# Reordering the opening of a fused clustered-attention and two-layer feed-forward kernel: squares, one-hot copies and a table load

## The chip, the cores and the metric

The kernel runs on one core of a Trainium2 chip. The metric is the device time of one execution in microseconds (us), smaller is better; the time given for a kernel is the median of several executions.

## The reference, cut to what matters

Clustered attention over 2 x 8 heads of 768 rows and 64 columns, then two feed-forward layers over the 1536 rows of 512 columns that the heads make up. Only the opening of the attention part is touched by the change.

```
q_n = q / (norm(q) + 1e-06);  k_n = k / (norm(k) + 1e-06);  c_n = centroids / (norm(centroids) + 1e-06)
q_assign = argmax(q_n @ c_n.T);  k_assign = argmax(k_n @ c_n.T)        # 16 centroids a head
mask = q_assign[:, None] == k_assign[None, :]
scores = where(mask, scale * q @ k.T, -1e9)
attn = exp(scores - max(scores));  attn = attn / (sum(attn) + 1e-09)
x = attn @ v                                                           # heads side by side: 1536 x 512
x = prelu(x @ w_in, alpha) @ w_out                                     # layer 1, d_ff 2048
x = rms_norm(x) * rms_g;  out = (silu(x @ w_gate) * (x @ w_val)) @ w_out2   # layer 2, d_ff 1536
```

## The kernel before

Heads are handled in eight pairs; q and k of a pair lie transposed in `raw[pr]` (128 partitions: two heads of 64 columns; index 0 is q, 1 is k; 768 rows each). Products that need full precision are made from a rounded part (`hi`) and its remainder (`lo`), which lie in `stages`. For each head two operand tiles are gathered by DMA: `op1` (partitions 0 to 63: `hi`; 64 to 79: a one-hot code of the row's cluster; 80 to 127: a part of `hi` of q and `lo` of k) and `op2`. A score tile on TensorE needs both; the one-hot rows make the mask, scaled by -2^60 on the q side.

Each engine works its instructions in the order in which the program writes them: an instruction that waits holds up all that stands behind it on its engine, and the DMAs issued by SyncE (SP) stand in one such order too. PSUM tiles named `ps_st` rotate through three buffers and `ps_pr` has one; a tile that gets a buffer again waits until the last reader of the tile before it is done. `ps_pv` and `ps_mx` have one buffer each, of two banks.

`setup` (L279 to L386) is the opening. It loads pairs 0 and 1 and does, for pair 0, everything up to the one-hot codes:

- roots of the centroids' sums of squares (`root`, tag `c`), transposed centroids (`spread`, L325, L328);
- squares of q and k (`prep_sq`, L469, ScalarE), `hi` and `lo` (`prep_hi` L608, `prep_lo` L614, VectorE);
- `warm` (L393): products of zeros, which only keep TensorE busy;
- `sims_mm` (L516): products of raw q and k with the centroids; `sims_copy` (L521) takes them out of PSUM, `sims_turn` (L527) transposes them back;
- `ss_rows` (L494): sums of squares by a product with ones, copied out (L496) and transposed (`ss_turn`, L503); `root` makes reciprocal norms of them: square root and an offset on ScalarE (L399, L400, and with `keep` a copy, L403), reciprocals on VectorE (L406 to L409);
- `prep_scale` and `prep_arg` (L543 to L565, VectorE): the argmax and the one-hot codes `oh`;
- the same products, sums and roots for pair 1, of which the VectorE part is left for later;
- a load of ScalarE's table set with the exponential (L376) and one small exponential (L378);
- `oht_direct(h)` (L577) for both heads of pair 0: 12 small products turn the codes into rows (L589; head 0 into `ps_pv` for k and `ps_mx` for q, head 1 into `ps_pr` and three `ps_st`), and ScalarE copies them into `op1` (k side L598, q side L600).

After that `plan` sets out slots from -12 on, each a list of steps sorted by a hand-written order. Slots -12 to -7 hold `max_tile` of phase 0: score products (L662) into `ps_pv` and `ps_mx` in turn, each followed by a maximum on VectorE (L666), with `max_split` (L671, L672) and `max_rows` (L690) behind; the first score tiles (`st_tile`, L712, L713, exponential L714) come in slots -7 and -5. In slot -12 SP also issues the second part of the operand gathers (`prep_dma_b(h, 2)`, L626, L630) and the loads of pair 2 (L454, L456).

Of the kernel before, what the change touches and what calls it, by code (L numbers as in the profile page):

```python
# [12 lines left out]
AF = mybir.ActivationFunctionType  # L13
ALU = mybir.AluOpType
# [4 lines left out]
BIG = float(2.0 ** 60)  # L19
# [170 lines left out]
def f(ap):  # L190
    return ap.bitcast(F32)
# [34 lines left out]
class Attention:  # L226
# [52 lines left out]
    def setup(self):  # L279

        nc, C, H, D = self.nc, self.C, self.H, self.D
        v, act, g = nc.vector, nc.scalar, nc.gpsimd
        n, rows = H * C, 2 * C
        cn = self.pre([n, 2, D], "cn")
        css = self.pre([n, 1], "css")
        self.sq0 = self.pre([128, D], "sq0")
        src = self.centroids.rearrange("h c d -> (h c) d")
        nc.sync.dma_start(out=cn, in_=src.unsqueeze(1).to_broadcast([n, 2, D]))
        for pr in range(2):
            for i in range(2, 4):  # L290
                self.load(pr, i)
        self.eps = self.pre([128, 2], "eps")
        self.hs = self.pre([128, 32], "hs")
        spare = self.pre([128, 1], "spare")
        for c, x in enumerate((1e-30, 1e-6)):
            g.memset(self.eps[:, c:c + 1], x)
        act.activation(out=spare, in_=self.eps[:, 0:1], func=AF.Sqrt)
        g.memset(self.cb0, 0.0)
        g.memset(self.hs, 0.0)
        for e in range(2):  # L300
            g.memset(self.hs[64 * e:64 * e + 64, e:e + 1], 1.0)
        g.memset(self.cb, 0.0)
        for t in self.mh:
            g.memset(f(t), 0.0)
        for c in range(C):
            g.memset(self.code[:, c:c + 1], float(C - c))
        pat = self.pre([128, 2 * C, 2, 2], "pat")
        g.memset(pat[:, :, 0], -BIG)
        g.memset(pat[:, :, 1], 1.0)
        for o2 in self.op2:  # L310
            g.memset(f(o2[64:66, 1, :]), 1.0)
        g.memset(self.ones, 1.0)
        g.memset(self.tiny, 1e-9)
        g.memset(self.low, 1.0)
        for i in range(4):
            g.memset(self.low[32 * i:32 * i + 1], 0.0)
        i = self.idf.rearrange("p (e g r) -> p g e r", e=2, r=32)
        hi, lo = (i[..., r:r + 1].to_broadcast([128, 2, 2, 64]) for r in range(2))
        g.tensor_tensor(out=self.sel, in0=hi, in1=lo, op=ALU.add)
        pat = pat.rearrange("p a i g -> p (a i g)")  # L320

        def spread(cb, w, copy):

            ps = self.bk.pr()
            nc.tensor.transpose(ps[:, :w], cn[:w].rearrange("p a d -> p (a d)"), self.idf[:w, :w])  # L325
            src = ps[:, :w].rearrange("p (j e c) -> p j e c", e=2, c=C)
            for e in range(2):
                copy(out=cb[64 * e:64 * e + 64, :, C * e:C * e + C], in_=src[64 * e:64 * e + 64, :, e, :])  # L328

        x = cn[:, 0, :]  # L330
        v.tensor_tensor_reduce(out=self.sq0[:n], in0=x, in1=x, scale=1.0, scalar=0.0, op0=ALU.mult, op1=ALU.add,
                               accum_out=css)
        steps, r = self.root(css, [n, 1], "c")
        self.warm(3, self.bk.pv)
        spread(self.cb0.unsqueeze(1), rows, v.tensor_copy)
        for step in steps:
            step()
        for i in range(2):
            self.prep_sq(0, i)
        self.prep_hi(0, 0)  # L340
        self.prep_lo(0, 0)
        for i in range(2):
            v.tensor_scalar(out=cn[:, i, :], in0=cn[:, i, :], scalar1=r, scalar2=None, op0=ALU.mult)
        self.prep_hi(0, 1)
        self.warm(6, self.bk.pv)
        rc = self.bk.st()
        for i in range(0, 128, rows):
            nc.tensor.matmul(rc[i:i + rows, 0:1], lhsT=self.idf[:rows, :rows], rhs=r[:rows], start=True, stop=True)
        act.copy(out=self.rc0, in_=rc[:, 0:1])
        ps = self.bk.pr()  # L350
        self.sims_mm(0, ps)
        self.prep_sq(1, 0)
        simc = self.sims_copy(0, ps, self.rc0)
        ssc = self.ss_rows(0, v.tensor_copy)
        for h in range(2):
            self.prep_dma_a(h)
        for h in range(2):
            self.prep_dma_b(h, 1)
        self.load_v(0)
        steps, rn = self.root(self.ss_turn(ssc), [128, self.T // 2, 4, 2], "n0")  # L360
        self.sims_turn(0, self.bk.st(), simc)
        spread(self.cb, n, act.copy)
        self.prep_sq(1, 1)
        for step in steps:
            step()
        self.norm[0] = None, rn
        self.prep_scale(0)
        for i in range(5):
            self.prep_arg(0, i)
        self.warm(3, self.bk.pv)  # L370
        ps = self.bk.st()
        self.sims_mm(1, ps)
        ssc = self.ss_rows(1, act.copy)
        self.simc[1] = self.sims_copy(1, ps, 1.0)
        self.norm[1] = self.root(self.ss_turn(ssc), [128, self.T // 2, 4, 2], "n1", True)
        act.add_instruction(mybir.InstLoadActFuncSet(name=nc.get_next_instruction_name(), act_func_set_id=EXP_AND_LN,  # L376
                                                     ins=[], outs=[]))
        act.activation(out=spare, in_=self.eps[:, 0:1], func=AF.Exp)  # L378
        self.warm(4, self.bk.pv)
        self.prep_lo(0, 1)  # L380
        for h in range(2):
            self.oht_direct(h)
        for i in range(2):
            self.prep_hi(1, i)
        v.tensor_tensor_reduce(out=pat, in0=pat, in1=self.idf, scale=1.0, scalar=0.0, op0=ALU.mult, op1=ALU.add,
                               accum_out=self.ohs)  # L386
# [190 lines left out]
    def oht_direct(self, h):  # L577

        nc, X = self.nc, self.T // 2
        if h:  # L580
            hi = [self.bk.pr(), self.bk.st()]
            ps = [[self.bk.st(), self.bk.st()], hi]
        else:
            ps = [b().rearrange("p a b -> p (a b)") for b in (self.bk.mx, self.bk.pv)]
            ps = [[b, b[:, self.HS:]] for b in ps]
        for i in (1, 0):
            for g in range(2):
                for x in range(X):
                    nc.tensor.matmul(ps[i][g][0:16, x * 128:(x + 1) * 128], lhsT=self.oh[0][:, x, h, :, i, g],  # L589
                                     rhs=self.idr, start=True, stop=True)  # L590
        o1 = self.op1[h][64:80]
        for i in (1, 0):
            cuts = ((0, 128), (128, self.S)) if not i else ((0, self.S),)
            parts = [(ps[i][g][:16, :self.HS], o1[:, i, sl]) for g, sl in self.halves()] if h else \
                [(ps[i][0][:16, a:b], o1[:, i, a:b]) for a, b in cuts]
            for src, dst in parts:
                if i:
                    nc.scalar.copy(out=dst, in_=src)  # L598
                else:
                    nc.scalar.activation(out=dst, in_=src, func=AF.Identity, scale=-BIG)  # L600

# [198 lines left out]
    def plan(self):  # L800
# [3 lines left out]
        def at(s, o, fn, *a):  # L804
            ev.setdefault(s, []).append((o, len(ev.get(s, [])), fn, a))
# [4 lines left out]
        for pr in range(self.NP):  # L810
# [8 lines left out]
                        at(b + to[0], to[1], fn, pr, n)  # L819
            h = 2 * pr  # L820
            if pr == 0:
                at(-12, -1, self.prep_dma_b, 0, 2)
                at(-12, 1, self.prep_dma_b, 1, 2)
            elif pr == 1:
                at(-5, 12, self.prep_dma_a, h)
                at(-4, 12, self.prep_dma_a, h + 1)
                at(5, 2.8, self.prep_dma_oh, h)
                at(5, 2.8, self.prep_dma_oh, h + 1)
                at(6, 2.8, self.prep_dma_b, h)
                at(6, 2.8, self.prep_dma_b, h + 1)  # L830
            else:
                for e in range(2):
                    at(b - 12, 2.5, self.prep_dma_a, h + e)
                    at(b - 12, 2.5, self.prep_dma_oh, h + e)
                    at(b - 11 + e, 2.5, self.prep_dma_b, h + e)
# [539 lines left out]
```

## Time and profile before

| | |
|---|---|
| time, median of 3 runs (lowest, highest) | 819.69 us (819.63, 819.71) |
| the profiled execution's own time | 819.63 us |
| its span in the profile | 817.9 us |
| instructions | 11705 |
| TensorE matmul busy | 809.6 us (99%) |
| VectorE busy | 623.7 us (76%) |
| ScalarE busy | 335.6 us (41%) |
| GpSimd busy | 362.1 us (44%) |

The span is the time between the first and the last recorded instruction; 1.7 us of the execution lie outside of it. A busy TensorE is one whose modelled matmul times leave no gap, and not one at its peak. Times of single rows are from the start of the span.

### The profile page before, as it was taken

The page shows a single profiled execution, that of the slowest core. Times are in us where ns is not written, and L with a number is a line of the kernel's source. Part 1 is how long each engine was busy: PE and PEld are TensorE (multiplying, and loading weights), DVE is VectorE, ACT ScalarE, POOL GpSimd, SP SyncE. Part 2 cuts the span into 40 slices and gives each one's busy share as a digit, 9 for nine tenths or more (in the row PEclk, how much of TensorE's full clock was granted, in tenths as well). Part 3 has the DMA queues.
Part 4 walks back from the last instruction along what each step waited for, and adds up shares of the span by engine and source line. Part 5 has one row for each costly group of instructions (what it writes and reads, how often), then busy time and mean ns, then how long its engine had stood idle before and what let it go on. Part 6 is the DMA issues. An engine that isn't in the chain of part 4 may idle for free.

```text
span 817.9 us, 11705 instructions
## 1 busy us (share of the span) xinstructions
PE 809.6 (99%) x4350; PEld 625.0 (76%) x4350; DVE 623.7 (76%) x1036; ACT 335.6 (41%) x652; POOL 362.1 (44%) x335
## 2 busy tenths in 40 slices
PE   8999999999999999999999999999999999999998
PEld 5565666666666888888888888888888888888887
DVE  6989999999998489999999977877555555555523
ACT  7655776666564333433434444432212221222110
POOL 3421221221213267786766772416465546554511
PEclk9999999999999999999999999999999999999999
DMA  8786655754532022232212220102121212121012
GB/s 206 201 229 181 132 154 161 171 111 115 133 114 79 1 77 78 78 103 65 88 59 75 77 78 1 51 1 78 52 77 54 76 52 77 57 73 51 1 52 103
DMA packets 23624, 74.03 MB, mean 91 GB/s; under 512 B 3600, under 2 KB 4752, under 8 KB 23568
## 3 DMA queue, kind: packets, MB, share of 16 engines
q1 hardware_dynamic: 23568, 73.29, 31.3%
q8 instruction: 34, 0.56, 0.3%
q14 instruction: 22, 0.18, 0.1%
HBM read 49.88 MB, written 3.15 MB: 65 GB/s over the span
## 4 chain that ended last, share of the span: by engine, by line
PE 96%; DVE 2%; DMA 1%; ACT 1%; issue 0%; SPq 0%; DVEq 0%; ACTq 0%
PE ps_st L1010 35%; PE ps_mx L1010 14%; PE ps_pv L1010 14%; PE ps_pv L728 8%; PE ps_pr L1010 5%; PE ps_st L712 4%; PE ps_st L713 4%; PE ps_sm L739 3%; PE ps_ma L662 3%; PE ps_mb L662 2%; DMA nat<-in_kn_dram 1%; DVE mx L666 1%; PE ps_pv L393 1%; PE ps_pr L516 1%; PE ps_pr L690 0%; PE ps_pr L782 0%
## 5 line engine op out<-in xcount | busy, mean ns | idle before, releaser
L1077 POOL TENSOR_TENSOR gl<-v,gh 128x512 fp32r<-128x512 f32 x68 | 96.0, 1412 | 143.8 <-ACT gh L1076 142.4
L1076 ACT CAST gh<-v 128x512 fp32r<-128x512 f32 x68 | 42.3, 622 | 151.9 <-DVE v L1073 83.3
L1073 DVE TENSOR_TENSOR v<-ps_st,t 128x512 f32<-128x512 f32 x36 | 24.9, 691 | 100.3 <-PE ps_st L1010 100.2
L714 ACT ACTIVATE p<-ps_st 128x384 f32<-128x384 f32 x192 | 85.3, 491 | 28.1 <-PE ps_st L713 26.6
L992 DVE SCALAR_TENSOR_TENSOR dec_a<-raw,dec_a 128x512 uint32<-128x512 uint32 x66 | 81.6, 1236 | 2.2
L728 PE MATMUL ps_pv<-p,vnat 128*64 128x384 f32 x384 | 72.6, 499 | 0.0
L1069 DVE SCALAR_TENSOR_TENSOR v<-v,alpha,t 128x512 f32<-128x512 f32 x45 | 53.0, 1177 | 21.9 <-ACT v L1068 21.8
L712 PE MATMUL ps_st<-op 128*128 128x384 f32 x192 | 67.8, 353 | 0.3 <-ACT oht L575 0.3
L1010 PE MATMUL ps_st<-x1h,stage 128*128 128x512 f32 x272 | 67.2, 389 | 0.0
L713 PE MATMUL ps_st<-op 82*128 82x384 f32 x192 | 65.0, 339 | 0.0
L1010 PEld LDWEIGHTS ps_st<-x1h,stage 128*128 128x128 f32 x272 | 51.1, 188 | 10.6
L1123 DVE TENSOR_TENSOR x<-ps_mx,x 128x1024 f32<-128x1024 f32 x36 | 43.9, 1220 | 18.7 <-PE ps_mx L1010 18.7
L664 DVE TENSOR_REDUCE mx<-ps_ma 128x1 f32<-128x384 f32 x90 | 49.7, 552 | 10.1 <-PE ps_ma L662 9.2
L798 POOL TENSOR_TENSOR x1l<-X,x1h 128x384 fp32r<-128x384 f32 x15 | 15.9, 1062 | 91.7 <-ACT x1h L795 91.7
L1010 PE MATMUL ps_st<-x1h,wvh 128*128 128x512 f32 x144 | 56.2, 390 | 0.0
L1010 PE MATMUL ps_st<-x1h,wvl 128*128 128x512 f32 x144 | 56.0, 389 | 0.0
L1010 PE MATMUL ps_st<-x1h,wih 128*128 128x512 f32 x132 | 51.6, 391 | 0.0
L1010 PE MATMUL ps_st<-x1h,wil 128*128 128x512 f32 x132 | 51.4, 389 | 0.0
L664 DVE TENSOR_REDUCE mx<-ps_mb 128x1 f32<-128x384 f32 x90 | 49.4, 549 | 0.1
L1123 DVE TENSOR_TENSOR x<-ps_pv,x 128x1024 f32<-128x1024 f32 x35 | 42.5, 1214 | 6.8 <-PE ps_pv L1010 6.8
L990 DVE TENSOR_SCALAR dec_a<-raw 128x512 uint32<-128x512 uint32 x66 | 47.6, 722 | 0.0
L995 DVE SCALAR_TENSOR_TENSOR dec_e<-raw,dec_e 128x512 f32<-128x512 uint32 x66 | 45.7, 692 | 2.3
(304 smaller groups left out, 1998.3 us busy)
## 6 DMA issues: line engine op xcount, KB each, us to landing
raw<-in_moe_w_out_dram SPq DMA_DIRECT2D x28, 512.0 KB, 3.5
op<-stage SPq DMA_DIRECT2D x32, 384.0 KB, 5.9
raw<-in_moe_w_in_dram SPq DMA_DIRECT2D x15, 512.0 KB, 3.6
raw<-in_moe_w_val_dram SPq DMA_DIRECT2D x12, 512.0 KB, 3.4
raw<-in_moe_w_gate_dram SPq DMA_DIRECT2D x12, 512.0 KB, 3.4
op<-stage SPq DMA_DIRECT2D x16, 288.0 KB, 5.9
raw<-in_qt_dram SPq DMA_DIRECT2D x8, 384.0 KB, 4.8
raw<-in_kt_dram SPq DMA_DIRECT2D x8, 384.0 KB, 5.1
```

Source lines behind the costliest of these rows:

```text
L664: nc.vector.tensor_reduce(out=mx[:, g, k:k + 1], in_=to, op=ALU.max, axis=AX.X)
L712: nc.tensor.matmul(ps, lhsT=o1[:, 1, ks], rhs=o1[:, 0, qs], start=True, stop=False)
L713: nc.tensor.matmul(ps, lhsT=o2[:, 1, ks], rhs=o2[:, 0, qs], start=False, stop=True)
L714: nc.scalar.activation(out=self.P[s][:, e], in_=ps, func=AF.Exp, scale=self.scale)
L728: nc.tensor.matmul(ps[64 * e:64 * e + 64], lhsT=self.vnat[ph // 2][:, e, t0 + y], rhs=P[y][:, e], start=t0 + y == 0, stop=t0 + y == T - 1)
L990: lambda: v.tensor_scalar(out=a, in0=top, scalar1=3, scalar2=0x3FFFFFFF, op0=ALU.logical_shift_left, op1=ALU.bitwise_and),
L992: lambda: v.scalar_tensor_tensor(out=a, in0=top, scalar=0xC0000000, in1=a, op0=ALU.bitwise_and, op1=ALU.bitwise_or),
L995: lambda: v.scalar_tensor_tensor(out=ef, in0=bot, scalar=2.0 ** -52, in1=ef, op0=ALU.mult, op1=ALU.mult),
L1010: self.nc.tensor.matmul(ps, lhsT=a, rhs=b, start=first and i == 0, stop=last and i == len(terms) - 1)
L1069: nc.vector.scalar_tensor_tensor(out=v, in0=v, scalar=self.nalpha[:, a], in1=t, op0=ALU.mult, op1=ALU.add)
L1077: nc.gpsimd.tensor_tensor(out=lo, in0=v, in1=f(hi), op=ALU.subtract)
L1123: nc.vector.tensor_tensor(out=dst, in0=ps, in1=dst, op=ALU.add)
```

## The change

For pair 0, the square of k is split: ScalarE squares the first 384 columns, VectorE the other 384. The sums of squares (`ss_rows(0)`) go to TensorE ahead of the products that spread the roots (L348) and of the centroids' products (`sims_mm(0)`), and ScalarE instead of VectorE copies them out. The scaling of the centroids moves from VectorE to ScalarE, `lo` of k from behind the one-hot codes to the first stretch of VectorE, the copy of the centroids' products (`sims_copy`) behind the roots' two ScalarE steps, and both squares of pair 1 behind the spread centroids. The second part of head 0's operand gather is issued ahead of the load of v. For the codes' rows: head 0's copies are split between ScalarE and VectorE and stand ahead of pair 1's roots, head 1's stand behind these roots (the second half of its k side on VectorE), and the table load comes after both.

```
--- before.py
+++ after.py
@@ setup
-        for i in range(2):
-            self.prep_sq(0, i)
-        self.prep_hi(0, 0)
-        self.prep_lo(0, 0)
-        for i in range(2):
-            v.tensor_scalar(out=cn[:, i, :], in0=cn[:, i, :], scalar1=r, scalar2=None, op0=ALU.mult)
-        self.prep_hi(0, 1)
+        self.prep_sq(0, 0)
+        self.prep_hi(0, 0)
+        sq, raw = self.nat[0][:, 1].rearrange("p t h d -> p (t h d)"), self.raw[0][:, 1]
+        (_, s0), (_, s1) = self.halves()
+        act.activation(out=sq[:, s0], in_=raw[:, s0], func=AF.Square)
+        v.tensor_tensor(out=sq[:, s1], in0=raw[:, s1], in1=raw[:, s1], op=ALU.mult)
+        self.prep_hi(0, 1)
+        for i in range(2):
+            act.activation(out=cn[:, i, :], in_=cn[:, i, :], func=AF.Identity, scale=r)
+        for i in range(2):
+            self.prep_lo(0, i)
         self.warm(6, self.bk.pv)
+        ssc = self.ss_rows(0, act.copy)
         rc = self.bk.st()
...
         self.sims_mm(0, ps)
-        self.prep_sq(1, 0)
-        simc = self.sims_copy(0, ps, self.rc0)
-        ssc = self.ss_rows(0, v.tensor_copy)
...
+        self.prep_dma_b(0, 2)
         self.load_v(0)
         steps, rn = self.root(self.ss_turn(ssc), [128, self.T // 2, 4, 2], "n0")
-        self.sims_turn(0, self.bk.st(), simc)
+        self.sims_turn(0, self.bk.st(), self.sims_copy(0, ps, self.rc0))
         spread(self.cb, n, act.copy)
-        self.prep_sq(1, 1)
+        for i in range(2):
+            self.prep_sq(1, i)
...
-        self.norm[1] = self.root(self.ss_turn(ssc), [128, self.T // 2, 4, 2], "n1", True)
+        ss = self.ss_turn(ssc)
+        self.warm(4, self.bk.pv)
+        self.oht_direct(0)
+        self.norm[1] = self.root(ss, [128, self.T // 2, 4, 2], "n1", True)
+        self.oht_direct(1)
         act.add_instruction(mybir.InstLoadActFuncSet(...))
         act.activation(out=spare, in_=self.eps[:, 0:1], func=AF.Exp)
-        self.warm(4, self.bk.pv)
-        self.prep_lo(0, 1)
-        for h in range(2):
-            self.oht_direct(h)
@@ oht_direct
+        cuts = (0, 128), (128, self.S)
         for i in (1, 0):
-            cuts = ((0, 128), (128, self.S)) if not i else ((0, self.S),)
-            parts = [(ps[i][g][:16, :self.HS], o1[:, i, sl]) for g, sl in self.halves()] if h else \
+            parts = [(ps[i][g][:16, :self.HS], o1[:, i, sl]) for g, sl in self.halves()] if h or i else \
                 [(ps[i][0][:16, a:b], o1[:, i, a:b]) for a, b in cuts]
-            for src, dst in parts:
+            for n, (src, dst) in enumerate(parts):
+                aside = n == (1 if i else 0) and (i or not h)
                 if i:
-                    nc.scalar.copy(out=dst, in_=src)
+                    (nc.vector.tensor_copy if aside else nc.scalar.copy)(out=dst, in_=src)
+                elif aside:
+                    nc.vector.tensor_scalar(out=dst, in0=src, scalar1=-BIG, scalar2=None, op0=ALU.mult)
                 else:
                     nc.scalar.activation(out=dst, in_=src, func=AF.Identity, scale=-BIG)
@@ plan
             if pr == 0:
-                at(-12, -1, self.prep_dma_b, 0, 2)
                 at(-12, 1, self.prep_dma_b, 1, 2)
```

## Rows read from the trace of the kernel before

**Rows 1.** The page, part 4: the chain that ended last, by engine.

```profile
PE 96%; DVE 2%; DMA 1%; ACT 1%; issue 0%; SPq 0%; DVEq 0%; ACTq 0%
```

**Rows 2.** The chain of waits, 0 to 60 us: start us, us, what.

```profile
3.33 2.86 PE ps_pv L393 x6
...
6.41 0.82 PE ps_pr L516 x8
7.22 0.70 PE ps_st L494 x8
...
8.56 0.55 PE ps_st L503 x3
...
13.71 1.28 ACT L376
...
15.24 0.79 ACT op L598
...
16.24 0.64 PE ps_pv L662 x2
...
16.90 2.70 DVE mx L666 x3
...
23.64 12.12 DMA nat<-in_kn_dram
...
36.65 0.47 ACT op L699
```

**Rows 3.** The timeline of ScalarE, 4 to 40 us: start, duration, instruction.

```profile
4.80 1.81 ACT L469 ACTIVATE nat<-raw 128x768 f32<-128x768 f32 x2 [1.12 <-DMA raw<-in_qt_dram]
...
7.72 0.56 ACT L521 ACTIVATE simc<-ps_pr,rc 128x384 f32<-128x384 f32 x1
...
9.46 0.32 ACT L400 ACTIVATE n_e<-n_y,eps 128x24 f32<-128x24 f32 x1
9.68 0.41 ACT L328 COPY cb<-ps_pr 64x64 f32<-64x64 f32 x2
10.11 0.84 ACT L469 ACTIVATE nat<-raw 128x768 f32<-128x768 f32 x1
11.89 0.48 ACT L496 COPY ssc<-ps_st 128x384 f32<-128x384 f32 x1 [0.94 <-PE ps_st L494]
...
13.54 0.16 ACT L403 COPY n_s<-ps_st 128x24 f32<-128x24 f32 x1
...
18.27 1.57 ACT L606 CAST stage<-raw 128x768 fp32r<-128x768 f32 x2
```

**Rows 4.** The timeline of VectorE, 4 to 30 us; in brackets the idle time before and its end.

```profile
7.95 0.56 DVE L496 COPY ssc<-ps_st 128x384 f32<-128x384 f32 x1 [0.47 <-PE ps_st L494]
9.46 0.30 DVE L406 RECIPROCAL n_a<-n_y 128x24 f32<-128x24 f32 x1 [0.95 <-ACT n_y L399]
```

**Rows 5.** The timeline of TensorE, 4 to 40 us: start, duration, instruction.

```profile
8.94 0.49 PE L527 MATMUL ps_st<-idf,simc 128*128 128x128 f32 x3
9.27 0.27 PE L325 MATMUL ps_pr<-idf,cn 128*128 128x128 f32 x1
...
12.72 1.17 PE L393 MATMUL ps_pv<-zero 128*128 128x512 f32 x4
14.21 0.52 PE L589 MATMUL ps_pv<-idr,oh 128*16 128x128 f32 x6 [0.31 <-DVE oh L565]
...
21.37 0.34 PE L712 MATMUL ps_st<-op 128*128 128x384 f32 x1
...
36.04 0.39 PE L690 MATMUL ps_pr<-idr,mh 128*64 128x128 f32 x3
```

**Rows 6.** Groups of instructions by line and shape, 4 to 24 us: ScalarE's L600.

```profile
L600 ACT ACTIVATE op<-ps_mx 16x640 fp32r<-16x640 f32 x1 | 0.7, 677 | 0.0
```

**Rows 7.** The timeline of SP's queue, 4 to 40 us.

```profile
15.47 0.56 SPq L626 DMA_DIRECT2D op<-stage  x1
```

**Rows 8.** Busy time by stretch, with granted clock, DMA share, GB/s at the end.

```profile
10.00:32.00 22.00, 19.69 (x132) 12.55 (x131) 19.53 (x45) 15.44 (x32) 5.50 (x11) 1.00 1.02 248
```

## Prediction

> **What bounds the kernel now.** I read the page's chain first, then the chain of waits over the first 60 us, then the timelines of the engines in the opening.
>
> The page puts 96% of the chain that ended last on TensorE [rows 1]. From about 39 us on its products follow each other to the end, and all engines work in written order. So what the opening gains or loses comes out at the end, less what later waits swallow. The reader should look at two things: when the first score product (L662) runs, and what swallows a shift behind it.
>
> The chain of the opening [rows 2]: zeros on TensorE from 3.33 to 6.19, centroids' products from 6.41, sums of squares from 7.22 to 7.92, a copy on VectorE at 7.95 [rows 4], transposes at 8.56. At the far end ScalarE loads the exponential's table at 13.71 for 1.28 us, copies head 0's code rows from 15.24, and the first score product starts at 16.24. The codes themselves were ready for TensorE at 14.21 [rows 5], so the copies began about 0.5 us after the first six products' end (14.73): that is what the load cost before. From 16.90 VectorE's maxima follow back to back, 0.9 us each. Then the chain shows a transfer from 23.64 to 35.76, the square that waited for it, and a row copy at 36.65.
>
> **The change, part by part.** All times are of the profiled execution (819.63 us, span 817.9); the median is 819.69, so its sums carry over as they are. What a measurement can tell from no change is about 0.2%, 1.64 us.
>
> *Pair 0's sums.* The two squares of 0.85 us ended at 6.61, so q is there at 4.80 and k at 5.76 [rows 3]. Half a square costs at most 0.48 on ScalarE (its copy of 384 columns [rows 3]) and 0.56 on VectorE [rows 4]: both halves are done by 6.33, when TensorE has just left the zeros (6.19). The sums take 0.70 plus at most 0.15 of waiting, to 7.0; ScalarE's copy ends at 7.5 instead of VectorE's at 8.52. But the products for the roots (0.22, from 6.19 to 6.41) and for the centroids (0.82) now stand between the sums and their transposes on TensorE: 7.0 + 1.04 = 8.0. The transposes start 0.55 earlier, not 1.0, and the root's second step (n_e) goes from 9.46 to 8.9.
>
> *VectorE's extra work.* It gets the half square (0.56) and `lo` of k (0.9 by the maxima of as many columns), 1.46 in all. It loses the copy (0.56) and the waits around it, 0.47 and 0.95 [rows 4], of which 1.43 are left when the reciprocal comes 0.55 earlier. The centroids' scaling leaves it too. So `lo` is hidden behind the wait for the square root; without that cover it would cost 0.9. I take 0; at worst 0.1.
>
> *The centroids' products.* Their copy now follows n_e, 0.22 after its start as L328 did before: 9.13, for 0.56 [rows 3], to 9.69 instead of 8.28. The transposes (0.49) end at 10.2, just when the roots are done, so VectorE's codes come 0.5 earlier: TensorE could have them at 13.7.
>
> *Pair 1.* Here the change pays. The transposes of the centroids end 0.6 after the start of the ones before [rows 5]: 10.3. Their two copies take 0.41, to 10.75 (before they began at 9.68). Both squares of pair 1 follow, 0.84 each with little overlap: 12.4, where before the second ended at 10.95 and the first lay in an earlier gap. The second half of pair 1's sums needs 0.35 to 0.5 more: 12.9, against 11.87. The copy and the transposes follow as before, 1.0 later, and the four products of zeros, which ended at 13.89, end at 14.9 [rows 5]. Only then come the code products: 14.9 instead of 14.21, although the codes are ready at 13.7.
>
> *Head 0's rows.* The six products for k end at 15.4 (0.52), the copies of both halves at 15.95 (0.56 the longer), the 128 columns of q on VectorE by 16.2, ScalarE's 640 (0.68 [rows 6]) at 16.5. The rows for the first score product are there at 16.2, as before. ScalarE is idle from about 13.8 to 15.4 now: the load and the small exponential (1.5) would have fitted in front of the copies. Moving them is worth nothing here.
>
> *Head 1's products.* They stand on TensorE ahead of the first score product, and the last three write the `ps_st` buffer that held pair 1's transposed sums. Its last reader is the copy L403, which now stands behind head 0's copies on ScalarE: 16.5, then 0.35 to n_e, 0.22 to L403, 0.16 [rows 2, 3], less 0.1 of overlap, is 17.1. The three products and the score product behind them follow: 17.3 instead of 16.24, 1.05 later. If that wait did not bind, TensorE would end the 24 products of 14.9 at 16.3 to 17.0 (each six between 0.35, an estimate from 0.52 less one product's run, and 0.52), so the shift lies between 0.1 and 1.05. I take the wait, since the order of the buffers and of ScalarE's steps is fixed by the text.
>
> *What lies behind.* The load is now between head 1's copies and the two casts of pair 1 (1.57 [rows 3]): about 18.3 to 19.8, casts to 21.4. The first score tile, 21.37 before, comes at about 22.4 and its exponential after it: hidden. The trace has the load at 1.28 us with the next instruction at its heels [rows 2]. The Trainium skill (ScalarE: Activation LUTs, What ACT_TABLE_LOAD costs) gives about 2.66 us for each switch, with a drain behind the load. By the page the casts would end near 22.8 and push the first rows' copy and exponential by about 1 us, to some 821.5; by the trace, which the sum follows, nothing.
>
> *Transfers.* Head 0's second gather goes from 15.47 [rows 7] to about 11, ahead of v. Its readers start at 21.37 before and 22.4 now; v is read later still. Nothing waits for either. All of SP's issues up to the casts of pair 1 come sooner, but the 16 DMA engines are at a share of 1.02 from 10 to 32 us [rows 8]: the end of this backlog moves only with its start, 0.3 to 0.7 earlier (`hi` of k comes that much sooner).
>
> *What swallows the shift.* The stretch from 16.9 to 36 is in order, so 1.05 arrives at 36: L690 ended at 36.43 [rows 5] and the row copy behind it waited for the late square until 36.65, which now is 0.2 of slack. 1.05 - 0.2 = 0.85 at the end: 819.69 + 0.85 = 820.5, span 818.7.
>
> **Rivals.**
> - *The buffer does not bind* or TensorE comes through pair 1 a little faster: a shift of 0.1 to 0.6 at the first score product, less 0.2: 819.6 to 820.1. For it: the trace of before shows no product that waits for L403, which ended at 13.70 there, before TensorE asked. Against it: the written order.
> - *The transfers set the stretch, on the other side.* The chain itself shows a transfer for 12.12 us up to 35.76. If the products have over 1 us of room in front of that square, the end follows the DMA backlog, 0.3 to 0.7 earlier: 819.0 to 819.4. It decides once products reach L690 no later than the square ends. Against it: L690 ended only 0.2 ahead of the row copy. The change would then do what its order suggests, at a size near the limit of measurement.
> - *TensorE's clock falls.* Its granted clock was 1.00 from 10 to 32 us [rows 8]; before 6.19 products of 512 columns took 0.48 each, later 0.29 or less [rows 2, 5]. TensorE now idles about 1.1 us (8.6 to 9.7) and 0.8 us (16.3 to 17.1), where the opening's chain had idled 0.64 at most between 6.19 and 9.1. If the clock fell, the some 5 us of products between 9.7 and 17.3 could take up to twice as long: 822 to 825. The Trainium skill (TensorE: Matmul & The Clock Gate, What's actually happening) says that the low level is the default and activity lifts it; no row before shows a fall.
> - *The load's place was the bound and pair 1 overlaps better than I sum*: first score product up to 0.9 earlier, 818.8 to 819.0, and not under 818 by any row.
>
> **How the numbers follow.** Forecast (0.5 to 1.1 later) 0.62; buffer not binding 0.15; transfers 0.12; clock or another wait 0.07; earlier first product 0.04. The likeliest gives 820.5. The range 819.2 to 821.2 leaves out the clock, the earlier product and half of the transfers' case, 0.17. Over 0.2% either way (under 818.05, over 821.33): faster 0.03; slower 0.09, from the clock and the forecast's tail; the rest, 0.88, within.
>
> **What would show it.** Right: transposes of pair 0's sums near 8.0; pair 1's second square ending near 12.4; ScalarE idle ahead of head 0's copies; TensorE waiting for ScalarE ahead of the last three code products; L662 near 17.3; the first table-bound exponential not waiting for the load; L699 near 37.5. Wrong: L662 before 16.2, or a slower TensorE product anywhere after 6.2 us, or a transfer that is waited for at 36 us with products idle.

## The result and the profile after

The changed kernel takes 825.01 us (median of 5, 824.60 to 825.15), the kernel before 819.71 us in the same job (819.63 to 821.00): 5.3 us more, a ratio of 1.006 with a 95% interval of 1.0047 to 1.0074. The span of the profiled execution went from 817.9 to 823.2 us. Lines have moved: the first score product L662 is L669 now, the row copy L699 is L706, the code copies L598 and L600 are L603, L605 and L607, the code products L589 are L593, sums of squares L494 are L498, the root's copy L403 is L407.

The page of the changed kernel, part 2: the span in 40 slices of 20.6 us, with the granted clock of TensorE in tenths.

```profile
PEclk9899999999999999999999999999999999999999
```

One slice is not at full clock: the second, from 20.6 us on. The stretches around it, from the same trace (granted clock is the third number from the end, DMA share the second):

```profile
17.30:19.20 1.90, 0.04 (x1) 0.04 (x2) 1.14 (x5) 1.42 (x5) 0.00 (x0) 1.00 0.95 246
19.20:20.60 1.40, 1.32 (x8) 0.93 (x8) 0.63 (x1) 1.40 (x4) 0.00 (x0) 1.00 1.12 206
20.60:27.50 6.90, 6.52 (x20) 5.86 (x21) 4.96 (x8) 3.17 (x5) 0.00 (x0) 0.51 1.02 305
```

TensorE was busy for 0.04 of 1.90 us ahead of 19.2; from 20.6 to 27.5 its granted clock was at the lower of its two levels (0.5, 1.2 GHz). The chain of waits of the changed kernel shows how it came to the idle stretch and what the clock then cost:

```profile
6.19 1.27 PE ps_st L498 x8
...
12.21 1.55 PE ps_st L498 x8
...
15.85 0.56 PE ps_pv L593 x6
...
16.43 0.47 ACT op L603
...
16.93 0.55 DVE op L603
17.48 0.21 DVE op L605
...
17.71 0.69 ACT op L607
...
18.41 0.29 ACT n_y L403
...
18.73 0.31 ACT n_e L404
19.04 0.07 ACT n_s L407
...
19.16 0.37 PE ps_st L593 x3
19.53 0.42 PE ps_pv L669 x2
...
20.98 1.01 PE ps_pv L669 x2
21.99 0.85 PE ps_pr L397 x2
22.85 0.64 PE ps_mx L669 x2
...
41.80 0.02 ACT op L706
```

The reader should see three things. Pair 0's sums of squares take 1.27 us where they took 0.70 [rows 2], and pair 1's 1.55 where the chain of the kernel before has 0.83:

```profile
11.04 0.83 PE ps_st L494 x8
```

The copies of head 0's rows stand one under the other, ScalarE, VectorE, VectorE, ScalarE, and the root behind them releases the last three code products. And from 20.98 to 26.94 the chain lies on TensorE itself, with zeros (L397) as part of it, where VectorE's maxima had set the pace [rows 2]. TensorE's timeline has the first score product (L669) and the first score tile (L719):

```profile
19.16 0.37 PE L593 MATMUL ps_st<-idr,oh 128*16 128x128 f32 x3 [1.87 <-ACT n_s L407]
19.37 0.57 PE L669 MATMUL ps_pv<-op 80*128 80x384 f32 x2
...
26.70 0.52 PE L719 MATMUL ps_st<-op 128*128 128x384 f32 x1
```

So the first score product is 3.1 us later (16.24 before [rows 2]) and the first score tile 5.3 (21.37 before [rows 5]). At the row copy it is 41.80 against 36.65 [rows 2], 5.15, and 5.3 at the end of the span.

### The profile page after: what moved, and what is told of

Read it like the earlier page. It is cut to its first block, busy times and chain, and to the rows that moved or that the text cites. A ratio compares the mean times of both kernels' runs of the same rounds, so it can differ in the third digit from the quotient of the medians.

```text
span 823.2 us, 11705 instructions
## 1 busy us (share of the span) xinstructions
PE 813.6 (99%) x4350; PEld 627.9 (76%) x4350; DVE 625.2 (76%) x1037; ACT 335.4 (41%) x653; POOL 363.1 (44%) x335
## 4 chain that ended last, share of the span: by engine, by line
PE 97%; DVE 1%; ACT 0%; issue 0%; DVEq 0%
PE ps_st L1016 34%; PE ps_mx L1016 14%; PE ps_pv L1016 14%; PE ps_pv L735 8%; PE ps_pr L1016 5%; PE ps_st L719 4%; PE ps_st L720 4%; PE ps_sm L746 3%; PE ps_ma L669 3%; PE ps_mb L669 2%; PE ps_pv L397 1%; PE ps_pr L520 1%; PE ps_pr L697 0%; PE ps_pr L789 0%; PE ps_mb L1016 0%; PE ps_ma L1016 0%
## 5 line engine op out<-in xcount | busy, mean ns | idle before, releaser
L719 PE MATMUL ps_st<-op 128*128 128x384 f32 x192 | 68.1, 355 | 0.1
```

The source lines that it names most:

```text
L719: nc.tensor.matmul(ps, lhsT=o1[:, 1, ks], rhs=o1[:, 0, qs], start=True, stop=False)
```

## The experiments

Each kernel was timed against the kernel before on one chip in the same job, and "+" is the difference of the two medians. TensorE's clock does not fall in every execution, nor for as long, so spreads are given where it matters. The openings of single executions also differ by some 0.4 us (code products from 15.61 us with the roots first, from 16.00 in the bank cut, whose program is the same up to there), so steps are compared below from the start of the code products where that matters.

**Roots first.** The changed kernel, with pair 1's roots back ahead of head 0's code products and copies.

```
         ss = self.ss_turn(ssc)
+        self.norm[1] = self.root(ss, [128, self.T // 2, 4, 2], "n1", True)
         self.warm(4, self.bk.pv)
         self.oht_direct(0)
-        self.norm[1] = self.root(ss, [128, self.T // 2, 4, 2], "n1", True)
         self.oht_direct(1)
```

> The changed kernel with one step moved back: pair 1's roots stand ahead of head 0's code products and copies again. Theory A (the buffer of pair 1's transposed sums, read last by L407 behind head 0's copies, holds TensorE for 1.87 us, and the idle stretch lets its clock fall): no wait ahead of the last three code products, first score product near 17.8 instead of 19.37, granted clock 1.00 throughout, time 821.0 to 821.6. Theory B (pair 1's later squares and sums do it, the clock falls for the earlier gaps at 9 and 14 us): the clock falls all the same, 823 or more. Theory C (the halves of the copies run one after the other): between 822.5 and 824.

821.60 us against 819.95, +1.65 (ratio 1.0015, 1.0005 to 1.0024), granted clock 0.999 or 1.000 in all ten executions. Its timeline:

```profile
15.20 0.16 ACT L407 COPY n_s<-ps_st 128x24 f32<-128x24 f32 x1
...
16.54 0.70 PE L593 MATMUL ps_st<-idr,oh 128*16 128x128 f32 x9
...
17.55 0.59 PE L669 MATMUL ps_pv<-op 80*128 80x384 f32 x2 [0.30 <-issue]
```

L407 is done before TensorE asks, all nine products run in one, the first score product comes 1.8 us sooner than in the changed kernel and the clock does not fall; the time is at the upper end of theory A's. This one step is 3.65 of the 5.3 us. Theory B fell: the gaps near 9 and 14 us (1.19 and 0.58) are still there.

**More zeros.** The changed kernel with eight products of zeros between head 0's and head 1's code products.

```
         self.oht_direct(0)
         self.norm[1] = self.root(ss, [128, self.T // 2, 4, 2], "n1", True)
+        self.warm(8)
         self.oht_direct(1)
```

> The changed kernel with eight more products of zeros between head 0's and head 1's code products, in the stretch in which TensorE waited for L407: nothing is earlier, but TensorE is not idle. Theory A (of the 5.3 us, 3.1 are the later first score product and 2.2 the fallen clock): first score product still near 19.4, clock 1.00, time 822.5 to 823.0. Theory B (the clock falls whatever TensorE does there): 824.5 or more.

822.88 against 820.06, +2.82 (1.0038, 1.0023 to 1.0053); in three of four executions the clock stayed at 1.000 (822.67 to 822.92), in one it was 0.997 (823.81).

```profile
18.71 0.16 ACT L408 COPY n_s<-ps_st 128x24 f32<-128x24 f32 x1
18.89 0.47 ACT L604 CAST op<-ps_pr 16x384 fp32r<-16x384 f32 x1
19.05 0.55 DVE L604 CAST op<-ps_st 16x384 fp32r<-16x384 f32 x1 [1.61 <-PE ps_st L594]
19.21 0.56 PE L670 MATMUL ps_pv<-op 80*128 80x384 f32 x2
```

The first score product (L670 here) is nearly as late as in the changed kernel (19.37), and 2.5 of the 5.3 us are gone, as theory A said. So the fallen clock itself was worth about 2.5 (2.1 by the two medians alone; they come from two jobs), and the later start 2.8.

**No zeros.** The kernel before without the seven products of zeros in slots -10 to -7.

```
-WARMS = ((-10, 0.3, 1), (-9, 0.3, 2), (-8, 0.3, 2), (-7, 0.3, 2))
+WARMS = ()
```

> The kernel before without the seven products of zeros in the slots -10 to -7; nothing else is changed, and the maxima on VectorE that set this stretch stay. Theory A (TensorE's clock falls when it idles in this stretch, and the fall alone costs 1 to 3 us): granted clock below 1.00 somewhere between 16 and 30 us, time 821 to 823. Theory B (the clock falls for the gaps before 16 us and not for these): clock as before, time 819.5 to 820.3.

822.52 against 820.06, +2.46 (1.0030, 1.0017 to 1.0044), mean clock 0.992 to 0.996 in all five. Two of its stretches:

```profile
18.00:20.00 2.00, 1.21 (x4) 0.59 (x4) 1.98 (x3) 1.99 (x4) 0.00 (x0) 1.00 1.02 187
...
22.00:24.00 2.00, 2.00 (x9) 1.78 (x8) 1.62 (x5) 0.86 (x2) 0.00 (x0) 0.50 0.96 283
```

Nothing but idle time was added, and the clock fell at nearly the same time (20.9 against 20.6 us) and in all five executions, against 3 of 20 of the kernel before in this job. The zeros of these slots are no decoration: they hold it.

**Whole copies.** The changed kernel with the copies unsplit on ScalarE, their place kept (the loop of the kernel before).

```
-        cuts = (0, 128), (128, self.S)
         for i in (1, 0):
-            parts = [... for g, sl in self.halves()] if h or i else \
+            cuts = ((0, 128), (128, self.S)) if not i else ((0, self.S),)
+            parts = [... for g, sl in self.halves()] if h else \
...
-            for n, (src, dst) in enumerate(parts):
-                aside = n == (1 if i else 0) and (i or not h)
+            for src, dst in parts:
                 if i:
-                    (nc.vector.tensor_copy if aside else nc.scalar.copy)(out=dst, in_=src)
-                elif aside:
-                    nc.vector.tensor_scalar(out=dst, in0=src, scalar1=-BIG, scalar2=None, op0=ALU.mult)
+                    nc.scalar.copy(out=dst, in_=src)
```

> The changed kernel with head 0's and head 1's copies all on ScalarE and unsplit as before, their place kept. Theory A: L407 still ends behind them, near 18.8, first score product near 18.9, the idle stretch of TensorE is 1.5 us and the clock falls: 824.3 to 824.9. Theory C (halves that share a PSUM bank run one after the other and cost more than a whole copy): first score product 0.9 or more earlier, clock kept, 822 or less.

823.54 against 819.95, +3.59 (1.0043, 1.0029 to 1.0056), from 821.87 at a clock of 1.000 to 825.28 at 0.996. L407 still ends near 19.1 in the profiled execution, which is the slowest of the five, and the idle stretch stays (1.43). No execution lies in theory A's range: one is above it, three are near 823.5, one is in theory C's. The first score product is no earlier in the timeline either, but this execution's opening is later:

```profile
16.26 0.55 PE L593 MATMUL ps_pv<-idr,oh 128*16 128x128 f32 x6
...
19.34 0.56 PE L666 MATMUL ps_pv<-op 80*128 80x384 f32 x2
```

From the start of the code products the first score product comes after 3.08 us here and after 3.52 in the changed kernel (15.85 to 19.37), and ScalarE ends head 0's copies after 2.12 instead of 2.55. So the split did not merely save nothing, it cost 0.4; theory C had the direction right, and put it at 0.9 or more.

**First part alone.** Split square, sums first, both squares of pair 1 late, `lo` of k and gather early; roots, load and whole copies as before. Against the changed kernel, besides the loop of the whole copies above:

```
-        ss = self.ss_turn(ssc)
-        self.warm(4, self.bk.pv)
-        self.oht_direct(0)
-        self.norm[1] = self.root(ss, [128, self.T // 2, 4, 2], "n1", True)
-        self.oht_direct(1)
+        self.norm[1] = self.root(self.ss_turn(ssc), [128, self.T // 2, 4, 2], "n1", True)
...
         act.activation(out=spare, in_=self.eps[:, 0:1], func=AF.Exp)
+        self.warm(4, self.bk.pv)
+        for h in range(2):
+            self.oht_direct(h)
```

> Only the first part of the change (split square, sums of squares first, pair 1's squares later, earlier lo of k and its gather); roots, table load and whole copies in the order of before. Theory A: code products near 15.9 as in the changed kernel, the table load hidden ahead of them, first score product near 18.1, clock 1.00, time 821.2 to 821.8. Theory B: the clock falls, 823.5 or more.

822.04 against 819.95, +2.09 (1.0029, 1.0020 to 1.0039), 821.15 to 824.54. In the profiled execution (821.26, clock 1.0) the code products start at 15.45, the load is hidden ahead of them, and the first score product comes at 17.74. The median is 0.2 above theory A's range, because the clock fell after all in 4 of 10 executions (0.996 to 0.998); the six others lie from 821.15 to 822.06.

**Second part alone.** Copies split, head 0's ahead of the roots, load last; squares and sums as before, `lo` of k behind the copies. Against the changed kernel, the opening of the kernel before comes back:

```
-        act.activation(out=sq[:, s0], in_=raw[:, s0], func=AF.Square)
-        v.tensor_tensor(out=sq[:, s1], in0=raw[:, s1], in1=raw[:, s1], op=ALU.mult)
...
+            self.prep_sq(0, i)
...
-        ssc = self.ss_rows(0, act.copy)
...
+        self.prep_sq(1, 0)
+        simc = self.sims_copy(0, ps, self.rc0)
+        ssc = self.ss_rows(0, v.tensor_copy)
...
         self.oht_direct(1)
+        self.prep_lo(0, 1)
```

> Only the second part (copies split, head 0's ahead of pair 1's roots, table load last); squares and sums as before, lo of k behind the code copies. Theory A: code products at 14.2, L407 ends near 17.4, first score product near 17.7, TensorE idle 1.7 us ahead of it and its clock falls: 822.5 to 823.5. Theory B: no later than before by more than 0.5, 819.3 to 820.2.

822.98 against 819.95, +3.03 (1.0035, 1.0025 to 1.0044), 821.15 at a clock of 1.000 to 824.76 at 0.994. L404 (the root's copy here) ends at 17.01, the first score product starts near 17.3, and the clock falls near 19. The time lies in theory A's range. The medians of the two parts, 2.1 and 3.0, come near the 5.3 of both; with spreads of over 3 us each this is no proof that the parts are independent.

**Bank cut.** Roots first, and head 0's k side cut at 512, the border of two PSUM banks.

```
-            parts = [... for g, sl in self.halves()] if h or i else [... for a, b in cuts]
+            parts = [... for g, sl in self.halves()] if h else \
+                [... for a, b in (((0, 512), (512, self.S)) if i else cuts)]
```

> The kernel with the roots first, and head 0's k side cut at column 512, the border of two PSUM banks, instead of at 384; its q side as it was. Theory A (copies of two engines out of one bank run one after the other): VectorE's 256 columns start together with ScalarE's 512, the 128 columns of q end near 17.0 instead of 17.45, first score product 0.2 to 0.5 earlier, time 0.2 to 0.4 less than with the roots first. Theory B (they wait for each other because both write one operand tile): VectorE still starts where ScalarE ends, near 16.8, and the time is 0.1 to 0.2 more.

820.97 against 820.06, +0.91 (1.0012, 1.0003 to 1.0021). Its median is 0.7 nearer to before than with the roots first, but that is another chip and job, and the first score product is no earlier in the profile: 17.90, which is 1.90 after the start of the code products, against 1.94 with the roots first. What the timeline settles is the order of the copies:

```profile
16.58 0.57 ACT L603 CAST op<-ps_pv 16x512 fp32r<-16x512 f32 x1 [0.84 <-PE ps_pv L593]
...
17.19 0.41 DVE L603 CAST op<-ps_pv 16x256 fp32r<-16x256 f32 x1 [2.59 <-ACT op L603]
```

VectorE still starts where ScalarE ends, so the bank is not the cause, and theory A as worded fell. Nor is it the operand tile, theory B: in the kernel with more zeros (above, 18.89 and 19.05) ScalarE and VectorE write halves of the same rows at the same time, out of two PSUM tiles. What is left is the source: in this program two engines that read one PSUM tile do so in turn, also where the columns lie in two banks. What the row shows is a wait that ends with ScalarE's copy (2.59 us), so the order is kept by a wait in the program; whether the chip could read faster side by side was not tried.

**Square early.** Roots first, and pair 1's square of q back in ScalarE's gap behind the copy `rc0`.

```
         act.copy(out=self.rc0, in_=rc[:, 0:1])
+        self.prep_sq(1, 0)
...
-        for i in range(2):
-            self.prep_sq(1, i)
+        self.prep_sq(1, 1)
```

> The kernel with the roots first, and pair 1's square of q back ahead of pair 0's roots, in a gap of ScalarE near 8. Theory A (the second half of pair 1's sums has to start after both squares and then takes a full 0.8, since four strips of TensorE work side by side only when all are ready): the sums end near 13.0, 0.5 to 0.8 earlier, and with them the code products, the first score product and the end: 0.5 to 0.8 less than with the roots first. Theory B (TensorE's own order through the centroids' transposes is the limit): 0.2 or less.

820.39 against 820.06, +0.33 (1.0003, 0.9994 to 1.0013): no difference from before. Against the roots first it is 1.3 less, more than theory A gave, but that is another job; against the bank cut, timed in the same job and no faster than the roots first from the code products on, it is 0.6, which is theory A. The sums and the first score product:

```profile
11.98 0.98 PE L498 MATMUL ps_st<-nat,hs 128*32 128x384 f32 x8
...
17.00 0.59 PE L669 MATMUL ps_pv<-op 80*128 80x384 f32 x2 [0.30 <-issue]
```

With both squares ready the eight products take 0.98 together; with the second square late the same eight take 1.57.

**Gather late.** Square early, and head 0's second gather back in slot -12.

```
-        self.prep_dma_b(0, 2)
...
+                at(-12, -1, self.prep_dma_b, 0, 2)
                 at(-12, 1, self.prep_dma_b, 1, 2)
```

> The kernel with the roots first and pair 1's square of q early, with head 0's second gather back in slot -12, behind the load of v. Theory A (the place of this gather costs and gives nothing): time within 0.3 of that kernel. Theory B (the gathers' order matters for the first score tile or the loads behind): 0.5 or more away from it.

820.70 against 819.93, +0.77 (1.0005, 0.9996 to 1.0014): not told from no change, and 0.4 from the kernel with the square early, between the two theories' bounds. Its place is worth little; whether 0.4 or nothing stays open.

**Copies by tile.** Square early, and ScalarE copies head 0's whole k side (one PSUM tile), VectorE only q's first 128 columns (the other); the four zeros ahead of the code products are gone. The loop of the copies is now:

```
             for n, (src, dst) in enumerate(parts):
                 if i:
                     nc.scalar.copy(out=dst, in_=src)
                 elif not h and not n:
                     nc.vector.tensor_scalar(out=dst, in0=src, scalar1=-BIG, scalar2=None, op0=ALU.mult)
                 else:
                     nc.scalar.activation(out=dst, in_=src, func=AF.Identity, scale=-BIG)
```

> The kernel with the roots first and pair 1's square of q early, and three edits more: head 0's k side is copied whole by ScalarE, VectorE takes only q's first 128 columns (another PSUM tile), and the four products of zeros ahead of the code products are gone. Theory A (two engines' copies out of one PSUM tile run one after the other, out of two tiles side by side): VectorE's 128 columns run beside ScalarE's 768, code products near 14.2, first score product 15.6 to 15.9, time 0.3 to 0.6 below the kernel before at the same clock. Theory B (something else is the limit): first score product 16.5 or later, time as before or more.

819.24 against 819.93, -0.69 (0.9990, 0.9981 to 0.9998), and no execution of eleven above 819.60: a version that beats both kernels, by less than 0.1% against the kernel before, which is within what was set as no change.

```profile
15.16 0.79 ACT L601 CAST op<-ps_pv 16x768 fp32r<-16x768 f32 x1
...
15.27 0.28 DVE L603 TENSOR_SCALAR op<-ps_mx 16x128 fp32r<-16x128 f32 x1 [0.55 <-PE ps_mx L592]
...
16.00 0.62 PE L667 MATMUL ps_pv<-op 80*128 80x384 f32 x2
```

Out of two tiles the engines run side by side. The three edits were not timed one by one: of the 1.0 us by which this first score product is earlier than with the square early, 0.7 is there at the code products (14.35 against 15.07), ahead of which the zeros are gone.

**Before, by tile.** The kernel before with the load behind the copies, the 128 columns on VectorE, `lo` of k behind the copies.

```
+        self.warm(4, self.bk.pv)
+        self.oht_direct(0)
+        self.oht_direct(1)
+        self.prep_lo(0, 1)
         act.add_instruction(mybir.InstLoadActFuncSet(name=nc.get_next_instruction_name(), act_func_set_id=EXP_AND_LN,
...
-        self.warm(4, self.bk.pv)
-        self.prep_lo(0, 1)
-        for h in range(2):
-            self.oht_direct(h)
...
+                elif not h and not n:
+                    nc.vector.tensor_scalar(out=dst, in0=src, scalar1=-BIG, scalar2=None, op0=ALU.mult)
```

> The kernel before with the table load and the small exponential behind both heads' code copies, q's first 128 columns on VectorE beside ScalarE's whole k side, and lo of k behind the copies; squares, sums, roots as before. Theory A (what the load cost is the 0.5 us between the first six code products and the first copy, and the 128 columns 0.2): first score product 15.5 to 15.7, time 0.4 to 0.7 below the kernel before at the same clock, if the gather that waits for lo of k does not become the limit. Theory B (the later gather holds the first score tiles): first score product as early, but the first score tile after 21.4, time as before or more.

819.70 against 819.93, -0.23 (1.0004, 0.9993 to 1.0015): no difference. The first score product starts at 15.73, 0.5 sooner than before, as theory A says, but theory A's time was missed, and not for theory B's gather. The chain of waits names what took it back:

```profile
15.21 0.28 DVE op L601
...
15.52 0.96 DVE stage L617
16.48 0.20 DVE pat L386
16.68 0.01 DVE ohs L386
16.69 2.61 DVE mx L669 x3
```

`lo` of k (L617) and the small reduction stand ahead of the maxima on VectorE, which start at 16.69 against 16.90 [rows 2]. In 4 of its 12 executions the clock fell too (0.998, 820.79 to 823.98).

## Why the prediction was wrong, point by point

It forecast 820.5 us and a range up to 821.2; the result is 825.01. The likeliest case had the right wait, L407, but put the shift of the first score product at 1.05 us where it is 3.13; and the rival that it gave 0.07, the clock, with a price of 822 to 825, came on top of this later start.

*Pair 0's sums: mis-sized.* Forecast done by 7.0, measured 7.46. The prediction took 0.70 for the eight from the chain before; here they take 1.27, though both half squares are done at 6.25. The change moved them from 7.05 to 6.12, where TensorE's products are still slow:

```profile
L498 PE MATMUL ps_st<-nat,hs x8: 513/716/849, 6.1 to 6.9; 128*32 128x384 f32 x8
...
L397 PE MATMUL ps_pv<-zero x9: 628/628/795, 1.4 to 5.6; 128*128 128x512 f32 x9
...
L397 PE MATMUL ps_pv<-zero x3: 395/397/478, 10.5 to 11.0; 128*128 128x512 f32 x3
```

(Shortest, median and longest in ns.) Pair 1's sums last 486 to 510 each. The zeros of the first 6 us last as long as those of the stretch at 0.5 (628 to 735). The granted clock of 6.1 to 7.5 us reads 1.00, but the trace has no record of the clock ahead of 6.98 us in this execution (6.47 in the kernel before), and time without a record counts as full. Slow products are not all of it: with the roots first, the sums last 486 to 511 each and the eight still take 1.22, from 6.00, since the four of k wait for their square until 6.35. Which share each has is open. Transposes of pair 0's sums start at 8.33 instead of 8.0.

*Codes: mis-sized, without effect.* The one-hot codes start at 13.67 on VectorE against 13.80 before, 0.13 earlier and not 0.5, as the copy of the centroids' products started at 9.45 instead of 9.13; TensorE asked for them only at 15.85.

*VectorE's extra work, load, transfers: right.* `lo` of both, 1.81 us from 6.71, ends at 8.52, ahead of the reciprocal at 9.23. The load lies at 20.36 and the first exponential comes at 27.58. No transfer is on the chain of the changed kernel up to 60 us: the rival on the other side fell. Of the about 2.66 us for a switch of tables (The Trainium skill, ScalarE: Activation LUTs, What ACT_TABLE_LOAD costs) the trace shows the load alone: 1.28, with the small exponential 0.01 behind it and no drain between.

*Pair 1: mechanism right, size off.* ScalarE's two squares run from 11.27 to 12.85 (forecast 12.4), later mostly because pair 0's sums were. The second half of the sums was put at 0.35 to 0.5 and took 0.91, to 13.76: half of them alone takes nearly as long as all eight where both squares are ready (0.98 in the square-early run). Code products start at 15.85 instead of 14.9.

*Head 0's rows: this step failed.* The prediction let ScalarE and VectorE copy halves side by side and ScalarE end at 16.5, 1.6 after the start of the code products. They ran in turn and ScalarE ended at 18.40, 2.55 after it. The bank-cut and by-tile runs show that it is the shared PSUM tile that puts them in turn, and whole copies on ScalarE alone took 2.12.

*Head 1's products: right.* The wait for L407 bound as told, 1.87 us; the terms above made it end at 19.11 instead of 17.1, and the first score product come at 19.37 instead of 17.3. Of these 2.0 us, 0.95 is there at the start of the code products, 0.95 comes from the copies in turn and 0.1 from the root's steps.

*The clock: named, but its chance and its place were wrong.* The prediction expected about 0.8 us of idle time at this place and weighed gaps one by one. The idle stretch became 1.87 us and the clock fell 1.5 us after it, on the products from 20.6 to 27.5 and not on those between 9.7 and 17.3, from which the price was made. Its own cost, 2.5, lies at the low end of the priced 2.3 to 5.3; that the total came out at the price's upper end is luck, since 2.8 of it are the later start. Which of the gaps it took cannot be told from one run. A gap of this length is not needed: in the run without zeros the clock fell with no gap of TensorE above 0.7 us between its first product and the fall. Filling this one kept the clock in three of four executions, and emptying the slots of before lost it in five of five. The Trainium skill (TensorE: Matmul & The Clock Gate, What's actually happening) has the low level as the default that activity lifts, and the run without zeros agrees (0.50 from 22 to 24 us).

*What swallows the shift: right at the row copy.* 5.33 at the first score tile, 5.15 at the row copy, where 0.2 was forecast to go; at the end of the span the difference is 5.3 all the same.

The sum: +2.8 for the later start and +2.5 for the clock. Taking the steps back one at a time gives 2.5 (zeros against idling, between two jobs) and then, within one job, 1.9 (the roots first, by the bank cut) and 0.6 (square early), leaving 0.3 that is not told from none. The place of the load alone, with `lo` of k behind the copies, gave nothing that can be measured.

## What to carry to other kernels

Splitting a copy between two engines saves nothing, and here cost 0.4 us, if both halves lie in one PSUM tile and the program makes its readers take turns: give each engine a tile of its own. A step that is moved to an earlier time may land where TensorE is still slow, so its cost is to be taken from rows of that time. Before a step is moved ahead of another on one engine, look up which buffers the second one releases, and which in-order engine stands still for them. In a stretch where TensorE idles often, an extra gap is to be priced at the lower clock as well, since the price (2.5 us here) can exceed the gap itself.

## What was not expected of the hardware

The clock falls in some executions of a program and not in others, and the time follows: with whole copies 821.87 at a mean clock of 1.000 and 825.28 at 0.996, and even the kernel before had 4 of 29 executions at 0.996 to 0.998, 821.4 to 822.5 against 819.2 to 820.4 for the rest. The start differs too: the first clock record of the thirteen traces, full in all, begins anywhere from 5.1 to 7.6 us. And the sums' small products (32 columns each), which overlap, hardly gain by being fewer: eight take 0.98 us when all are ready and 1.57 when the last four come late, and those four alone take 0.9.
